# An attention and expert kernel on one core: attention loads released by TensorE's progress, values a step sooner, early weights behind the gathers

## The chip, the cores and the metric

The kernel runs on one core of a Trainium2 chip. The metric is device time in microseconds (us) of one execution; smaller is better. Single launches of one program differ a little, so a time is given as the median of several runs with the lowest and the highest.

## The reference

Eight batches of eight heads, 576 positions, 64 numbers a head. Heads 0 to 3 attend to the last 32 positions (local), heads 4 to 7 to every 32nd position (strided). The rows of the result are tokens, and each goes through one of eight experts.

```python
scores = scale * np.matmul(q, k.transpose(0, 1, 3, 2))
mask_local = (rel >= 0) & (rel < stride)
mask_strided = (rel >= 0) & (pos[None, :] % stride == pos[:, None] % stride)
...
attn = attn / (np.sum(attn, axis=-1, keepdims=True) + 1e-09)
return np.matmul(attn, v).astype(np.float32)
...
logits = x @ w_gate + modality_bias[modality_id]
e_idx = np.argmax(logits, axis=1)
for e in range(E):
    h = np.maximum(x[mask] @ w1[e], 0.0)
    out[mask] = gate_w[mask, None] * (h @ w2[e])
```

## The kernel before

**Two stages.** The attention stage takes about the first 157 us. Behind it the expert stage runs 18 slots of 256 tokens and one half slot; per slot TensorE does the same eight pieces (up, L924, and down, L938), each in three products of high and low parts, and weights come in by indirect DMAs on GpSimd's queue (L811).

**Attention in units and steps.** `units` (L968 to 975) holds 32 units in turn: `Local` (two batches of one local head) and `Strided` (two strided heads of one batch). The loop at L1045 makes one step for each n and works on several units at once. In step n stand the scores of unit n (L380 and L387 for a local, L476 for a strided one), the transposes of the softmaxed scores of unit n-2 (`turn`, L217), the masks of unit n+1 (L368, L469) and the products with the values of unit n-3 (`values`: L420 and L432, or L520). Small pieces of other work are put in between: `pop` runs the joining of finished heads and the routing (`finish_pair`, `route`: tiles xl, xs, lg), and `slow` issues, one each time, scatters of finished token rows to the DRAM table xd (L646), and later the first gathers of tokens and weights (`early`, L989). Between L1041 and L1075 TensorE's order is the order of the code; the other engines' order comes from a scheduler.

**Loads.** They are issued on SyncE's queue (SP), which does one after the other and stands still where one has to wait. A unit's queries and keys are two DMAs of 64 rows (`load_qk`, L324: even partitions at L326, odd ones at L327; tile lqk of a local unit, sqk of a strided one). Each kind has two buffers, so unit n+3 writes the buffer of unit n-1 and waits for its scores. Values are in tile vv for a local unit, also with two buffers, and vs for a strided one. Up to the seventh local unit (`SPREAD`, L31) vv comes in four parts, of which GpSimd copies two on (L360, L361); later ones come from array vl in two. vs is one DMA of 72 rows of 4 KB. In step n stand first the queries and keys of unit n+3, and behind them the values of unit n-1 (L1046 to L1049).

**Waits written by hand.** `paced(ins)` (L219) makes an instruction wait for the TensorE instruction in `recent`, the last one that a helper has noted there: a transpose, a product with values, or a score of a strided unit. Before the change only small work, the scatters and `early` use it. `early` issues weights 0, the two halves of token gather 0, weights 1, the two halves of gather 1, one each time that `slow` comes by.

Of the kernel before, what the change touches and what calls it, by code (L numbers as in the profile page):

```python
# [11 lines left out]
F32 = mybir.dt.float32  # L12
# [8 lines left out]
P = 128  # L21
# [89 lines left out]
def _layout(q, k, v, moe_modality_id, moe_w_gate, moe_modality_bias, moe_w1, moe_w2):  # L111
    q, k, v = (np.asarray(t, np.float32) for t in (q, k, v))

    def local_t(t):
        return t[:, :4].reshape(NBP, 2, 4, S, D).transpose(0, 2, 1, 4, 3).reshape(NBP, 4, 2, D, 18, 32)

    qt, kt = local_t(q), local_t(k)
    vr = v[:, :4].reshape(NBP, 2, 4, 18, 32, D).transpose(0, 2, 1, 3, 4, 5)  # L120
    qkl = np.zeros((NBP, 4, 2, D, 37, 32), np.float32)
    win = np.zeros((NBP, 4, 2, 64, 20, D + 1), np.float32)
    vb = np.zeros((NBP, 4, 2, 32, 9, 2, D + 1), np.float32)
    ve = np.zeros((NBP, 4, 64, 2, D + 1), np.float32)
    vf = np.zeros((NBP, 4, 32, D + 1), np.float32)
    win[..., D] = vb[..., D] = ve[..., D] = vf[..., D] = 1
    vf[..., :D] = vr[:, :, 1, 1]
    for bb in range(2):
        for i in range(18):
            blk = _block(i, bb)  # L130
            qkl[:, :, bb, :, i] = qt[:, :, bb, :, blk]
            qkl[:, :, bb, :, 19 + i] = kt[:, :, bb, :, blk]
            w = win[:, :, i % 2, :, 2 * (i // 2) + bb] if i < 16 else win[:, :, 0, :, 2 * i - 16 + bb]
            w[:, :, 32:, :D] = vr[:, :, bb, blk]
            vb[:, :, i % 2, :, i // 2, bb, :D] = vr[:, :, bb, blk]
            if blk:
                qkl[:, :, bb, :, 18 + i] = kt[:, :, bb, :, blk - 1]
                w[:, :, :32, :D] = vr[:, :, bb, blk - 1]
        for lo in range(2):
            ve[:, :, 32 * lo:32 * lo + 32, bb, :D] = vr[:, :, bb, _block(16 + lo, bb)]  # L140
    qkl = np.stack([qkl[:, :, 1], np.concatenate([qkl[:, :, 0, :, 18:], qkl[:, :, 0, :, :18]], axis=-2)], axis=2)
    qkl = qkl.reshape(NBP, 4, P, 37 * 32)
    vl = win.reshape(NBP, 4, P, 20 * (D + 1))
    vb, ve = vb.reshape(NBP, 4, 2, 32, 18 * (D + 1)), ve.reshape(NBP, 4, 64, 2 * (D + 1))

    def strided_t(t):
        t = t[:, 4:].reshape(B, 2, 2, 18, 32, D).transpose(0, 1, 2, 5, 4, 3)
        return np.ascontiguousarray(t).reshape(B, 2, 2, D, S)

    qs, ks = strided_t(q), strided_t(k)  # L150
    qks = np.stack([np.concatenate([qs[:, :, 1], ks[:, :, 1]], axis=-1), np.concatenate([ks[:, :, 0], qs[:, :, 0]], axis=-1)],
                   axis=2).reshape(B, 2, P, 2 * S)

    vs = v[:, 4:].reshape(B, 2, 2, 18, 4, 2, 4, D).transpose(0, 1, 6, 3, 4, 5, 2, 7)
    vs = np.ascontiguousarray(vs).reshape(B, 2, 72, 1024)

    w1 = np.asarray(moe_w1).reshape(E, 4, P, 8, P).transpose(0, 3, 2, 1, 4).reshape(E, 8, P, 512)
    w2 = np.asarray(moe_w2).reshape(E, 8, P, DM)
    w = np.concatenate([w1, w2], axis=-1).reshape(E, 4, 2, P, 1024).transpose(0, 1, 3, 2, 4).reshape(E * 4 * P, 2048)

    wg = np.zeros((P, 4, 32), np.float32)
    wg[:, :, :E] = np.asarray(moe_w_gate).reshape(4, P, E).transpose(1, 0, 2)
    mod = np.ascontiguousarray(moe_modality_id).astype(np.int64).view(np.int32).reshape(NT, 2)[:, 0]
    mod = mod.reshape(36, P).transpose(1, 0)
    mb = np.broadcast_to(np.asarray(moe_modality_bias).reshape(1, 2 * E), (P, 2 * E))
    cf, cb, tok = _constants()
    nul = np.zeros((1, ROW), np.int32)
    nul[0, DM] = NT
    arrays = {
        "qkl": qkl, "vl": vl, "vb": vb, "ve": ve, "vf": vf, "qks": qks, "vs": vs, "w": w,  # L170
        "wg": wg.reshape(P, 4 * 32), "mod": mod, "mb": mb, "cf": cf, "cb": cb, "tok": tok, "nul": nul.view(np.float32),
    }
    return {n: np.ascontiguousarray(t) for n, t in arrays.items()}
# [20 lines left out]
def attention_moe(ctx: ExitStack, tc: tile.TileContext, a, out):  # L194
    nc = tc.nc
# [125 lines left out]
    for t in ets:  # L321
        nc.vector.memset(t[:], 0.0)

    def load_qk(t, nk, src):  # L324
        w = src.shape[1]
        nc.sync.dma_start(t[0:P:2, nk:nk + w], src[0:64])  # L326
        nc.sync.dma_start(t[1:P:2, 0:w], src[64:128])  # L327

    class Local:

# [1 line left out]
        def __init__(self, bp, h, xt):  # L332
            self.bp, self.h, self.xt, self.n = bp, h, xt, 4 * bp + h

        def load(self):
            n = self.n
            self.qk = lqk[n % 2]
            load_qk(self.qk.rearrange("p x i q -> p (x i q)"), S + 32, a["qkl"][self.bp, self.h])

        def load_values(self):  # L340
            n = self.n
            self.vv = vv = vvs[n % 2]
            w, at = D + 1, (self.bp, self.h)
            for dst, src in (
                (vv[32:64, 0:18, :], a["vb"][*at, 0]),
                (vv[96:128, 0:16, :], a["vb"][*at, 1, :, 0:16 * w]),
                (vv[0:64, 18:20, :], a["ve"][*at]),
                (vv[0:32, 1, :], a["vf"][*at]),
            ) if n < SPREAD else (
                (vv[:, 0:16, :], a["vl"][*at, :, 0:16 * w]),  # L350
                (vv[0:64, 16:20, :], a["vl"][*at, 0:64, 16 * w:]),
            ):
                ins = nc.sync.dma_start(dst, src)
                if n < 2:
                    pin(ins)

        def spread_values(self):
            vv = self.vv
# [12 lines left out]
        def scores(self):  # L371
            n, q, kd = self.n, self.qk[:, 0, 19:37, :], self.qk[:, :, 0:19, :]
            self.ex = ex = lp.tile([P, 9, 64], F32, tag="ex", name=f"ex{n}")
            for half, sp in enumerate(self.sp):
# [9 lines left out]
                if half:  # L384
                    for u in range(4):
                        i = 16 + u // 2
                        nc.tensor.matmul(  # L387
                            sp[32 * u:32 * u + 32, 256:320], q[:, i, :],
                            kd[:, u % 2, i:i + 2, :].rearrange("p i q -> p (i q)"),
                            start=False, stop=True, skip_group_check=True,  # L390
                        )
                mx = lp.tile([P, 5], F32, tag="mx", name=f"mx{n}{half}")[:, :gn]
                nc.vector.tensor_reduce(mx, sp.rearrange("p (g c) -> p g c", g=gn), AX.X, ALU.max)
                e = ex[:, 4 * half:4 * half + gn, :]
# [54 lines left out]
    class Strided:  # L449
# [2 lines left out]
        def __init__(self, b, pr, xc):  # L452
            self.b, self.pr, self.xc, self.n = b, pr, xc, 2 * b + pr

        def load(self):
            n = self.n
            self.qk = sqk[n % 2]
            load_qk(self.qk.rearrange("p i q -> p (i q)"), S, a["qks"][self.b, self.pr])

        def load_values(self):  # L460
            n = self.n
            self.vs = lp.tile([72, 8, 2, D], F32, tag="vs", name=f"vs{n}")
            ins = nc.sync.dma_start(self.vs.rearrange("p g h d -> p (g h d)"), a["vs"][self.b, self.pr])
            if n < 2:
                pin(ins)

        def masks(self):
            self.s = pa(f"ss{self.n}")[:, :288]
# [45 lines left out]
        def values(self):  # L514
            n, eb, vs, b = self.n, self.eb, self.vs, self.b
            for g2 in range(2):
                ot = pa(f"ot{n}{g2}")[:, :288]
                for u in range(4):
                    for h in range(2):
                        recent[:] = [nc.tensor.matmul(  # L520
                            ot[64 * h:64 * h + 64, 72 * u:72 * u + 72],
                            vs[:, 4 * g2 + u, h, :],
                            eb[:, 4 * (2 * h + g2) + u, :, :].rearrange("p t q -> p (t q)"),
                            start=True, stop=True, skip_group_check=True,
                        )]
                base = (b % 2) * S
                dst = self.xc[:, base:base + S].rearrange("p (q r) -> p r q", r=32)[:, 16 * g2:16 * g2 + 16, :]
                nc.scalar.copy(dst, ot.rearrange("p (r q) -> p r q", r=16))
# [459 lines left out]

    def early():  # L989
        for k in range(2):  # L990
            yield
            pin(paced(weights(tables[0][1], 0, k)))
            yield
            n, t, i, xrows = plan[k]
            for xt, ins in token_halves(n, tables[t][0], i, xrows):
                gathered[k] = xt
                pin(paced(ins))
                yield

    def slow():  # L1000
        while calm and next(calm[0], calm) is calm:
# [35 lines left out]

    nu = len(units)
    for i in range(3):
        units[i].load()  # L1040
    man = tc.manual_schedule(engines={mybir.EngineType.PE})  # L1041
    man.__enter__()
    units[0].masks()
    setup = routing_setup()
    for n in range(nu + 3):  # L1045
        if n + 3 < nu:  # L1046
            units[n + 3].load()
        if 1 <= n <= nu:
            units[n - 1].load_values()  # L1049
        if 2 <= n <= nu + 1 and not n % 2:  # L1050
            units[n - 2].spread_values()
        if n < nu:
            units[n].scores()
            if n % 2:
                slow()
            pop(MIDS)
        if 2 <= n <= nu + 1:
            units[n - 2].turn()
        slow()
        if n + 1 < nu:  # L1060
            units[n + 1].masks()
# [83 lines left out]
```

## Time and profile before

| | |
|---|---|
| median of 3 runs | 602.03 us (599.36 to 603.37) |
| the profiled execution, its own time | 597.48 us |
| its span, first to last instruction | 595.4 us |
| mean granted TensorE clock | 0.977 |
| TensorE matmul busy | 564.8 us, 95% |
| VectorE, ScalarE, GpSimd busy | 426.1, 358.7, 244.7 us |
| TensorE busy from 0 to 160 us | 138.2 us |
| TensorE busy from 200 to 560 us | 359.96 of 360 us |

The page gives, for each engine, the share of the span in which it worked (PE is TensorE's matmuls, PEld its weight loads, DVE VectorE, ACT ScalarE, POOL GpSimd, SP SyncE). A chain of waits goes back from the last instruction to whatever released each one; "issue" in it is time in which the engine waited for nothing that the profile shows. A table of windows gives for a stretch of time each engine's busy time and its number of instructions in brackets, then the granted TensorE clock (PEclk, 1.00 is full), the busy share of the 16 DMA engines and the GB/s that they moved. A timeline of a queue (SPq) lists when each DMA was issued, not when its data came.

### The profile page before, as it was taken

To read this page: it belongs to the slowest core of one execution; us is meant where nothing else is said; L and a number is where in the kernel's file an instruction comes from. 1 tells how busy PE (TensorE), PEld (TensorE's weight loads), DVE (VectorE), ACT (ScalarE), POOL (GpSimd) and SP (SyncE) were. 2 spreads that over 40 slices of the span, in tenths; PEclk is the share of its full clock that TensorE was granted. 3 is DMA by queue.
4 is the path that set the end of the run, shared out by engine and by line. 5 is a ranking of instruction groups with operands and counts; after the bars stand their busy time and mean duration, and the time that the engine had idled before them with its cause. 6 is when DMAs were issued, how large, how long until landed. Compare 5 with 4: busy or idle time off the path is not lost.

```text
span 595.4 us, 15277 instructions
## 1 busy us (share of the span) xinstructions
PE 564.8 (95%) x6040; PEld 494.4 (83%) x6040; DVE 426.1 (72%) x1050; ACT 358.7 (60%) x739; POOL 244.7 (41%) x219
## 2 busy tenths in 40 slices
PE   6979888989998999999999999999999999999995
PEld 3767776767887989999899899999998998998984
DVE  6776662957969997767767777777777677677541
ACT  3455664657866566666666666665665666666641
POOL 1413240143757786642543533533534533332220
PEclk9789997989999999999999999999999999999998
DMA  8988895897788855955934823413403438200621
GB/s 275 250 220 217 250 344 189 276 341 258 262 215 210 259 164 164 236 184 129 250 119 125 248 98 74 108 36 73 109 21 87 109 119 252 71 16 22 244 91 38
DMA packets 66669, 100.57 MB, mean 169 GB/s; under 512 B 47775, under 2 KB 49055, under 8 KB 63008
## 3 DMA queue, kind: packets, MB, share of 16 engines
q0 software_dynamic: 19744, 58.57, 29.7%
q1 hardware_dynamic: 46560, 40.56, 27.0%
q8 instruction: 49, 0.80, 0.6%
q10 hardware_dynamic: 288, 0.41, 0.2%
q14 instruction: 28, 0.23, 0.1%
HBM read 121.74 MB, written 19.43 MB: 237 GB/s over the span
## 4 chain that ended last, share of the span: by engine, by line
PE 85%; issue 5%; DVE 4%; DMA 3%; ACT 2%; POOL 1%; SPq 0%; POOLq 0%; ACTq 0%
PE h L924 33%; PE o L938 32%; PE o L420 3%; PE s L380 3%; PE ot L520 3%; PE lg L571 2%; PE xs L217 2%; PE t L217 2%; PE ss L476 1%; PE xl L217 1%; PE ts L217 1%; DMA vv<-in_vb 1%; ACT wh L959 1%; DVE wl L960 1%; DMA lqk<-in_qkl 1%
## 5 line engine op out<-in xcount | busy, mean ns | idle before, releaser
L960 DVE TENSOR_TENSOR wl<-raw,wh 128x512 fp32r<-128x512 f32 x288 | 185.9, 686 | 85.0 <-ACT wh L959 84.9
L959 ACT CAST wh<-raw 128x512 fp32r<-128x512 f32 x288 | 164.0, 618 | 91.4 <-PE o L938 89.6
L924 PE MATMUL h<-xl,wh 128*128 128x256 f32 x576 | 162.1, 282 | 1.4 <-DVE xl L912 1.4
L924 PE MATMUL h<-xh,wh 128*128 128x256 f32 x576 | 163.0, 284 | 0.2 <-ACT xh L911 0.2
L924 PE MATMUL h<-xh,wl 128*128 128x256 f32 x576 | 162.8, 283 | 0.0
L811 POOL DMA_INDIRECT raw<-in_w,wi x72 | 92.7, 1287 | 162.4 <-DVE wl L960 154.1
L924 PEld LDWEIGHTS h<-xl,wh 128*128 128x128 f32 x576 | 108.8, 189 | 8.1 <-DVE xl L912 2.1
L938 PE MATMUL o<-wh,hh 128*128 128x512 f32 x288 | 114.6, 398 | 0.0
L924 PEld LDWEIGHTS h<-xh,wh 128*128 128x128 f32 x576 | 108.4, 189 | 7.1 <-issue 0.6
L938 PE MATMUL o<-wl,hh 128*128 128x512 f32 x288 | 113.6, 395 | 0.0
L938 PE MATMUL o<-wh,hl 128*128 128x512 f32 x288 | 112.2, 395 | 0.0
L924 PEld LDWEIGHTS h<-xh,wl 128*128 128x128 f32 x576 | 108.3, 188 | 0.9
L927 ACT ACTIVATE hh<-h 128x256 fp32r<-128x256 f32 x144 | 55.2, 384 | 55.0 <-PE h L924 52.7
L929 DVE SCALAR_TENSOR_TENSOR hl<-h,hh 128x256 fp32r<-128x256 f32 x144 | 60.3, 419 | 12.5 <-ACT hh L927 12.3
L646 POOL DMA_INDIRECT xd<-xt,posi x36 | 40.4, 1121 | 59.1 <-DVE sms L496 16.5
L938 PEld LDWEIGHTS o<-wh,hl 128*128 128x128 f32 x288 | 53.7, 188 | 11.8
L938 PEld LDWEIGHTS o<-wh,hh 128*128 128x128 f32 x288 | 54.3, 188 | 7.6
L938 PEld LDWEIGHTS o<-wl,hh 128*128 128x128 f32 x288 | 54.3, 189 | 5.8
L946 POOL DMA_INDIRECT out<-y,le x36 | 46.2, 1283 | 24.0 <-ACT y L945 16.1
L792 POOL DMA_INDIRECT fx<-xd,li x36 | 39.2, 1090 | 23.6 <-issue 8.5
L409 ACT COPY et<-t 64x512 f32<-64x512 f32 x32 | 18.5, 579 | 21.1 <-PE t L217 20.7
L420 PEld LDWEIGHTS o<-vv,et 128*64 128x64 f32 x512 | 19.0, 152 | 13.4 <-issue 10.1
(183 smaller groups left out, 687.9 us busy)
## 6 DMA issues: line engine op xcount, KB each, us to landing
lqk<-in_qkl SPq DMA_DIRECT2D x32, 296.0 KB
sqk<-in_qks SPq DMA_DIRECT2D x32, 288.0 KB
vv<-in_vl SPq DMA_DIRECT2D x9, 520.0 KB
vs<-in_vs SPq DMA_DIRECT2D x16, 288.0 KB
raw<-in_w,wi POOLq DMA_INDIRECT x72, 2.5
vv<-in_vb SPq DMA_DIRECT2D x7, 146.2 KB
vv<-in_vb SPq DMA_DIRECT2D x7, 130.0 KB
vv<-in_vl SPq DMA_DIRECT2D x9, 65.0 KB
```

The source lines that it names most:

```text
L217: recent[:] = [nc.tensor.transpose(dst, src, ident)]
L420: recent[:] = [nc.tensor.matmul(os[bb][64 * jj:64 * jj + 64, bb + k, :], et[:, 2 * (k // 2) + bb, 2 * (k % 2) + jj, :, :].rearrange("p g q ...
L646: scattered(bp, paced(nc.gpsimd.indirect_dma_start(xd[0:(bp + 1) * T2, :], IOA(ap=posi[:, i:i + 1], axis=0), xt[:, i, :], None)))
L792: yield xt, fetches(min(xrows // T2, NBP) - 1, nc.gpsimd.indirect_dma_start(xt[:, h, :], None, xd[0:xrows, :], IOA(ap=li[:, s, h:h + 1], a ...
L811: return nc.gpsimd.indirect_dma_start(raws[j].rearrange("p f c -> p (f c)"), None, a["w"], IOA(ap=wi[:, s, j:j + 1], axis=0), bounds_check ...
L924: recent[:] = [nc.tensor.matmul(hp, w[:, a1], x[:, c, :], start=(k == 0), stop=(k == 11))]
L927: nc.scalar.activation(hh[:], hp, AF.Relu)
L929: nc.vector.scalar_tensor_tensor(hl[:], hp, 0.0, hh.bitcast(F32), ALU.max, ALU.subtract)
L938: nc.tensor.matmul(os[h], hx[:, m], w[:, 512:1024], start=(f == 0 and i == 0), stop=(f == 7 and i == 2))
L946: outs.add(nc.gpsimd.indirect_dma_start(out, IOA(ap=le[:, h, 0:1], axis=0), y[:], None, bounds_check=NT - 1, oob_is_err=False))
L959: nc.scalar.copy(wh[:, c], raw[:, c])
L960: nc.vector.tensor_tensor(wl[:, c], raw[:, c], wh[:, c].bitcast(F32), ALU.subtract)
```

## The change

It does five things. The queries and keys are issued one half at a time: for unit n+3 the even partitions behind the scores of unit n, the odd ones behind `turn` of unit n-2, both `paced` (from step 1 on; in step 0 unit 3 is loaded at once). The values of unit n are issued at the head of step n instead of step n+1, ahead of the queries and keys, and `paced` from the third unit of each kind on. The late local values come in two DMAs of 64 rows instead of one of 128. vs is padded from 72 to 80 rows, of which the products read 72. `early` issues both token gathers ahead of both weights. So that `paced` follows the scores of local units too, the last score now sets `recent`.

```diff
-    vs = np.ascontiguousarray(vs).reshape(B, 2, 72, 1024)
+    vs = np.concatenate([vs.reshape(B, 2, 72, 1024), np.zeros((B, 2, 8, 1024), np.float32)], axis=2)
...
-    def load_qk(t, nk, src):
+    def load_qk(t, nk, src, x):
         w = src.shape[1]
-        nc.sync.dma_start(t[0:P:2, nk:nk + w], src[0:64])
-        nc.sync.dma_start(t[1:P:2, 0:w], src[64:128])
+        if x:
+            return nc.sync.dma_start(t[1:P:2, 0:w], src[64:128])
+        return nc.sync.dma_start(t[0:P:2, nk:nk + w], src[0:64])
...
-                (vv[:, 0:16, :], a["vl"][*at, :, 0:16 * w]),
+                (vv[0:64, 0:16, :], a["vl"][*at, 0:64, 0:16 * w]),
+                (vv[64:128, 0:16, :], a["vl"][*at, 64:128, 0:16 * w]),
...
                 if n < 2:
                     pin(ins)
+                else:
+                    paced(ins)
...
-                        nc.tensor.matmul(
+                        recent[:] = [nc.tensor.matmul(
                             sp[32 * u:32 * u + 32, 256:320], q[:, i, :],
...
-            self.vs = lp.tile([72, 8, 2, D], F32, tag="vs", name=f"vs{n}")
+            self.vs = lp.tile([80, 8, 2, D], F32, tag="vs", name=f"vs{n}")
...
     def early():
         for k in range(2):
+            n, t, i, xrows = plan[k]
+            for xt, ins in token_halves(n, tables[t][0], i, xrows):
+                yield
+                gathered[k] = xt
+                pin(paced(ins))
+        for k in range(2):
             yield
             pin(paced(weights(tables[0][1], 0, k)))
-            yield
-            n, t, i, xrows = plan[k]
-            for xt, ins in token_halves(n, tables[t][0], i, xrows):
-                gathered[k] = xt
-                pin(paced(ins))
-                yield
...
     for i in range(3):
-        units[i].load()
+        for x in range(2):
+            units[i].load(x)
...
     for n in range(nu + 3):
-        if n + 3 < nu:
-            units[n + 3].load()
-        if 1 <= n <= nu:
-            units[n - 1].load_values()
+        if not n:
+            for x in range(2):
+                units[3].load(x)
+        if n < nu:
+            units[n].load_values()
         if 2 <= n <= nu + 1 and not n % 2:
             units[n - 2].spread_values()
         if n < nu:
             units[n].scores()
+            if n and n + 3 < nu:
+                paced(units[n + 3].load(0))
             if n % 2:
                 slow()
             pop(MIDS)
         if 2 <= n <= nu + 1:
             units[n - 2].turn()
+        if n and n + 3 < nu:
+            paced(units[n + 3].load(1))
         slow()
```

The first place is SyncE's queue at the start of the program; lqk_84 and lqk_85 are the two buffers of the local units, sqk_86 and sqk_87 those of the strided ones, vv_90 the first buffer of local values. Before:

```order
L326 DMA sqk_87<-in_qks 64x1152
L327 DMA sqk_87<-in_qks 64x1152
L326 DMA lqk_84<-in_qkl 64x1184
L327 DMA lqk_84<-in_qkl 64x1184
L353 DMA vv_90<-in_vb 32x1170
L353 DMA vv_90<-in_vb 32x1040
```

And of the change:

```order
L328 DMA sqk_87<-in_qks 64x1152
L327 DMA sqk_87<-in_qks 64x1152
L355 DMA vv_90<-in_vb 32x1170
L355 DMA vv_90<-in_vb 32x1040
L355 DMA vv_90<-in_ve 64x130
L355 DMA vv_90<-in_vf 32x65
L467 DMA vs_192<-in_vs 80x1024
L328 DMA lqk_84<-in_qkl 64x1184
```

The first values moved ahead of the second load of lqk_84, which has to wait for unit 0's scores; the first vs moved there too.

The second place is the same queue in a later step, with what each row waits for (PE is a TensorE instruction, DMAHW with a number an earlier DMA on one of eight semaphores). Before:

```order
L353 DMA vv_91<-in_vl 128x1040 [waits DMAHW4_49,PE_49]
L353 DMA vv_91<-in_vl 64x260 [waits DMAHW5_49,PE_49]
L326 DMA lqk_85<-in_qkl 64x1184 [waits DMAHW6_49,PE_49]
L327 DMA lqk_85<-in_qkl 64x1184 [waits DMAHW7_49]
L463 DMA vs_1841<-in_vs 72x1024 [waits DMAHW0_49,PE_49]
L326 DMA sqk_87<-in_qks 64x1152 [waits DMAHW1_49,PE_49]
L327 DMA sqk_87<-in_qks 64x1152 [waits DMAHW2_49]
```

And of the change:

```order
L355 DMA vv_91<-in_vl 64x1040 [waits DMAHW4_49,PE_49]
L355 DMA vv_91<-in_vl 64x1040 [waits DMAHW5_49]
L355 DMA vv_91<-in_vl 64x260 [waits DMAHW6_49,PE_49]
L328 DMA sqk_86<-in_qks 64x1152 [waits DMAHW7_49,PE_49]
L327 DMA sqk_86<-in_qks 64x1152 [waits DMAHW0_49,PE_49]
L467 DMA vs_1706<-in_vs 80x1024 [waits DMAHW1_49,PE_49]
L328 DMA lqk_85<-in_qkl 64x1184 [waits DMAHW2_49,PE_49]
L327 DMA lqk_85<-in_qkl 64x1184 [waits DMAHW3_49,PE_49]
```

Every second half now has a TensorE instruction of its own to wait for, and values of a later unit stand beside the same queries and keys. There are nine more DMAs, the second parts of the late local values.

The third place is GpSimd's queue at the end of the attention stage; raw is a tile of weights, fx_0 and fx_1 are the first two gathers of tokens. Before:

```order
L811 DMA raw_2704<-in_w,wi_2225 128x2048 [waits DVE_49,PE_49]
L792 DMA fx_0_2787<-xd,li_2217 128x528 [waits DVE_49,PE_49]
L792 DMA fx_0_2787<-xd,li_2217 128x528 [waits PE_49]
L811 DMA raw_2904<-in_w,wi_2225 128x2048 [waits PE_49]
L792 DMA fx_1_2975<-xd,li_2217 128x528 [waits PE_49] x2
```

And of the change:

```order
L798 DMA fx_0_2619<-xd,li_2223 128x528 [waits DVE_49,PE_49]
L798 DMA fx_0_2619<-xd,li_2223 128x528 [waits PE_49]
L798 DMA fx_1_2796<-xd,li_2223 128x528 [waits PE_49] x2
L817 DMA raw_2914<-in_w,wi_2231 128x2048 [waits PE_49]
L817 DMA raw_2985<-in_w,wi_2231 128x2048 [waits PE_49]
```

The first weights moved behind four gathers, the second behind two. TensorE's rows are the same, in the same order, up to the first expert slots, where the scheduler has put some pieces of neighbouring slots the other way round.

More of the change, by code (lines that the diff above doesn't have):

```diff
@@ L333, in __init__, with load @@
             self.bp, self.h, self.xt, self.n = bp, h, xt, 4 * bp + h
-        def load(self):
+        def load(self, x):
             n = self.n
             self.qk = lqk[n % 2]
-            load_qk(self.qk.rearrange("p x i q -> p (x i q)"), S + 32, a["qkl"][self.bp, self.h])
+            return load_qk(self.qk.rearrange("p x i q -> p (x i q)"), S + 32, a["qkl"][self.bp, self.h], x)
         def load_values(self):
@@ L390, in scores @@
                             start=False, stop=True, skip_group_check=True,
-                        )
+                        )]
                 mx = lp.tile([P, 5], F32, tag="mx", name=f"mx{n}{half}")[:, :gn]
@@ L453, in __init__, with load @@
             self.b, self.pr, self.xc, self.n = b, pr, xc, 2 * b + pr
-        def load(self):
+        def load(self, x):
             n = self.n
             self.qk = sqk[n % 2]
-            load_qk(self.qk.rearrange("p i q -> p (i q)"), S, a["qks"][self.b, self.pr])
+            return load_qk(self.qk.rearrange("p i q -> p (i q)"), S, a["qks"][self.b, self.pr], x)
         def load_values(self):
             n = self.n
-            self.vs = lp.tile([72, 8, 2, D], F32, tag="vs", name=f"vs{n}")
+            self.vs = lp.tile([80, 8, 2, D], F32, tag="vs", name=f"vs{n}")
             ins = nc.sync.dma_start(self.vs.rearrange("p g h d -> p (g h d)"), a["vs"][self.b, self.pr])
@@ L465, in load_values @@
                 pin(ins)
+            else:
+                paced(ins)
         def masks(self):
@@ L521, in values @@
                             ot[64 * h:64 * h + 64, 72 * u:72 * u + 72],
-                            vs[:, 4 * g2 + u, h, :],
+                            vs[0:72, 4 * g2 + u, h, :],
                             eb[:, 4 * (2 * h + g2) + u, :, :].rearrange("p t q -> p (t q)"),
```

## The prediction

> **What bounds the kernel now.** I read the page first, then a table of windows by stage, then the chain of waits over the attention stage, and for its odd pieces the windows between them. The stages first (us; then busy time of PE, PEld, DVE, ACT, POOL with the number of instructions; granted clock, DMA share, GB/s):
>
> ```profile
> 0.00:160.00 160.00, 138.20 (x3302) 111.11 (x3303) 109.41 (x406) 91.86 (x211) 50.08 (x64) 0.93 0.85 262
> 200.00:560.00 360.00, 359.96 (x2289) 325.51 (x2288) 271.68 (x514) 227.37 (x445) 162.52 (x130) 1.00 0.46 128
> ```
>
> From 200 us on TensorE never rests and has its full clock: nothing there can be won by moving loads. The attention stage is different. TensorE rests 160 - 138.2 = 21.8 us in it, and its clock is 0.93. So the question is where those 21.8 us lie. The chain of waits (start, length, what) has the answer:
>
> ```profile
> 9.41 6.33 DMA vv<-in_vb
> 15.90 1.04 POOL vv L360
> 17.00 1.00 POOL vv L361
> 18.04 2.00 PE o L420 x30
> ...
> 31.47 1.37 issue
> ...
> 43.08 1.64 issue
> ...
> 49.39 1.15 issue
> ...
> 70.53 1.67 issue
> ...
> 86.47 0.61 PE o L420 x15
> 87.08 3.98 issue
> 91.06 1.24 PE o L420 x17
> ```
>
> ```profile
> 114.27 0.83 issue
> ...
> 119.36 1.71 issue
> ...
> 132.84 0.65 issue
> ```
>
> One wait is for data: the first values, issued at 9.41, let TensorE go on at 18.04. All the others are called "issue", 13.00 us in sum, and they break off in the middle of a group: at 87.08 fifteen of 32 equal products are done, the other seventeen follow 3.98 us later, though all read the same tiles. No tile was missing. What was missing shows when one counts instructions (PE and PEld) between such breaks:
>
> ```profile
> 43.08:49.39 6.31, 4.67 (x125) 4.01 (x126) 4.51 (x13) 2.95 (x8) 2.04 (x2) 1.00 0.92 243
> 70.53:87.08 16.55, 14.88 (x378) 12.52 (x377) 11.16 (x36) 10.56 (x26) 7.36 (x8) 0.90 0.93 308
> 87.08:119.36 32.28, 26.93 (x630) 21.00 (x631) 19.37 (x92) 16.52 (x40) 4.66 (x6) 0.89 0.76 245
> ```
>
> 125 + 126 = 251; 755 is 3 times 252; 1261 is 5 times 252. Breaks come only at whole multiples of about 251 instructions. On the page stands a queue with as many packets as that makes:
>
> ```profile
> PE 564.8 (95%) x6040; PEld 494.4 (83%) x6040; DVE 426.1 (72%) x1050; ACT 358.7 (60%) x739; POOL 244.7 (41%) x219
> q8 instruction: 49, 0.80, 0.6%
> ```
>
> 12,080 instructions through 49 packets are 247 each. So TensorE's program itself comes by DMA, a block of some 250 instructions at a time, and a break is a block that came late. In the expert stage a block lasts about 20 us (4,577 instructions in 360 us), in attention 6,605 instructions are 26 blocks in 160 us, 6.1 us each: only there can it be late. And there the DMA engines are full; the break of 3.98 us falls into the fullest stretch:
>
> ```profile
> 77.00:92.00 15.00, 11.02 (x319) 9.47 (x315) 7.79 (x23) 8.80 (x21) 5.76 (x6) 0.95 0.97 348
> 20.00:140.00 120.00, 106.19 (x2583) 86.41 (x2582) 77.05 (x279) 69.70 (x164) 33.92 (x37) 0.92 0.84 255
> ```
>
> Each long rest has a second price, a halved clock soon after (the 0.50 in the last columns):
>
> ```profile
> 15.50:22.20 6.70, 5.46 (x84) 4.26 (x82) 4.55 (x12) 1.19 (x3) 2.83 (x3) 0.50 0.95 265
> 32.60:35.80 3.20, 2.95 (x38) 2.24 (x38) 2.21 (x5) 2.87 (x8) 0.29 (x1) 0.50 0.69 191
> 73.50:76.80 3.30, 3.30 (x48) 2.65 (x38) 2.86 (x10) 1.31 (x3) 2.10 (x2) 0.50 0.93 254
> 90.60:97.30 6.70, 6.24 (x66) 3.79 (x70) 1.15 (x6) 0.76 (x2) 1.25 (x2) 0.50 0.70 246
> 121.30:124.60 3.30, 3.30 (x68) 2.80 (x64) 1.74 (x13) 0.00 (x0) 0.95 (x1) 0.50 1.02 344
> ```
>
> Half of the busy time in each is lost: 2.7, 1.5, 1.65, 3.1 and 1.65 us. They follow the start and the breaks of 1.37, 1.67, 3.98 and 1.71 us; those of 1.64, 1.15, 0.83 and 0.65 have none behind them.
>
> **The change part by part.** *The start.* SyncE's queue shows why the first values are late (issue times):
>
> ```profile
> 5.89 0.56 SPq L327 DMA_DIRECT2D sqk<-in_qks  x1
> 8.25 0.47 SPq L326 DMA_DIRECT2D lqk<-in_qkl  x1
> ```
>
> The queue stands from 6.45 to 8.25, because lqk's second load waits for unit 0's scores, and the values are behind it. Now they stand ahead of it and can go out at about 7.0, 2.4 us sooner; with the same 6.33 us under way, and GpSimd's two copies of 2.1 us, the values are ready near 15.5. TensorE's own work ahead of them ends then at 16.3:
>
> ```profile
> 15.63 0.69 PE L368 MATMUL s<-cb_sb 128*128 128x256 bf16 x2
> ```
>
> So the products begin at 16.3 instead of 18.04: -1.7 us. With 2 us less rest the second half of that slow-clock period should go, 1.35 us. I take -3; bounds 0 (another engine holds TensorE until 18) and -5 (the whole period of 2.7 us goes and the block that follows comes in time).
>
> *The blocks.* Before, a buffer that comes free lets both halves out at once:
>
> ```profile
> 81.48 0.47 SPq L326 DMA_DIRECT2D lqk<-in_qkl  x1
> 82.01 0.63 SPq L327 DMA_DIRECT2D lqk<-in_qkl  x1
> ```
>
> A pair is 2 x 64 x 4,736 B = 0.606 MB, at the 348 GB/s of that stretch 1.74 us of DMA time; values add up to 0.6 MB, as much again. Afterwards a half, 0.87 us, is let out behind the scores, the other half some TensorE work later, the values at the head of the step. A block that is asked for behind such a burst then waits 0.87 us (the other half) to 2.6 us (half and values) less. I take 1 us, near the low end, since the scatters on GpSimd's queue, which are let out as before, stay in the way. Each break is shortened by 1 us or to nothing: 1.37, 1.64, 1.15, 1.67, 3.98 and 1.71 by 1, 0.83 and 0.65 altogether, 7.5 us in sum. Bounds: 0, if the depth of the queue does not matter, and 13.0, all breaks.
>
> *The clock.* The breaks of 1.37, 1.67 and 1.71 us become 0.4 to 0.7, the size of those that cost no clock: 1.5 + 1.65 + 1.65 = -4.8 us. The one of 3.98 stays near 3 and keeps its 3.1. Bounds 0 and -7.9.
>
> *Given back.* The same bytes go in less time. From 20 to 140 us the DMA engines are busy for 0.84 x 120 = 101 us; with 12 us less that is 0.93 of the stretch, and where it is 0.97 already there is little to win. I put +2 on it, an estimate between 0 (a spread load queues less) and +10 (TensorE gains only until the engines are full, which gives most of it back).
>
> *Loads one step later.* Queries and keys of unit n+3 were let out by the scores of unit n-1, and are now by work of step n. A step is 4.8 us, by these two pieces, twelve pairs of steps apart:
>
> ```profile
> 23.26 1.15 PE ot L520 x32
> ...
> 138.18 1.15 PE ot L520 x32
> ```
>
> The second half still has two and a half steps, 12 us, against the 6.33 us that the values took under a full queue. I cost it at 0; that cover is what the slower rival takes away. Behind a waiting half on SyncE's queue stand only the next values, which have three steps and more.
>
> *Small parts, at 0 together.* Nine more DMAs on SyncE's queue are nine issues of about 0.6 us while it waits for TensorE anyway. vs grows by 32 KB, 0.1 us of DMA time, sixteen times. [...]
>
> *The early weights.* They go out in the place of the second gather:
>
> ```profile
> 147.36 0.94 POOL L792 DMA_INDIRECT fx<-xd,li  x1 [0.92 <-PE rk L638]
> 149.17 0.94 POOL L792 DMA_INDIRECT fx<-xd,li  x1 [0.86 <-PE ts L217]
> ```
>
> ```profile
> 157.17 4.27 ACT wh L959 x8
> ```
>
> A tile of weights is 1.05 MB, 4 us at the stage's 262 GB/s: the first lands near 152, the second near 156, and ScalarE's casts begin at 157.17 and come to the second tile 2.1 us later. I take 0; if the scatters behind take turns with them, up to +3.
>
> **Sum:** -3 - 7.5 - 4.8 + 2 = -13.3 us against the profiled execution's 597.48, so 584.2. That execution lies 4.55 us under the median of the runs, 602.03, so I forecast 588.7, rounded to 589.
>
> **The rivals.** *The depth of the queue does not matter.* If a block's packet has to pass only what is in the engines, it waits as before as long as any load runs; then only the start is won, 602 - 3 = 599. For it: a break of 1.64 us at 43.08 stands where 243 GB/s, no peak, are moved. Against it: the longest break is in the fullest stretch, and none is in the expert stage. [...]
>
> *The DMA engines become the bound.* The breaks go, but the loads can't follow, and half of the gain returns as waits for lqk or sqk: -13.3 becomes -6, 596. For it: 0.97 in the fullest stretch. Against it: 0.84 over the whole.
>
> *Slower: the engines run dry between releases.* A load is let out only when TensorE gets there. From 20 to 140 us they are idle 0.16 x 120 = 19.2 us; there are 25 steps with three releases, 75. If each leaves a gap of over 19.2 / 75 = 0.26 us, loads fall behind TensorE and it waits for lqk and sqk. At 0.4 us, less than one issue of 0.47, that is 30 - 19.2 = +10.8, less 3 at the start: 610. For it: 0.89 or more of DMA share in several windows. Against it: loads that are late pile up, and a queue that has piled up leaves no gaps.
>
> **How the numbers follow.** The forecast gets 0.60 (its own range 579 to 597, from all breaks and most of the clock to a third of both), the full engines 0.12, depth without effect 0.18, gaps 0.10. A measurement of this kernel can tell about 1%, 6 us, from no change. Faster by over 1%, under 596: the forecast nearly whole, 0.59, and half of the full engines, 0.06: 0.65. Within 1%: 0.01 + 0.06 + 0.18 = 0.25. Slower: 0.10. The range 579 to 603 leaves out the gaps, 0.10, and about 0.08 at its ends.
>
> **What would show it.** Right: the first products with values begin at 16 to 17 us; the "issue" pieces of the attention stage fall from 13.0 to 4 to 7 us, still at multiples of some 251 instructions; the clock from 0 to 160 us rises to 0.95 or more; the expert stage begins some 12 us sooner and runs at the same pace. Wrong: breaks of the same size (depth does not matter), or PE waits whose releaser is a DMA of lqk, sqk, vv or vs after 20 us (gaps or full engines), or a rest at the first slot that ends with raw (the early weights).

## The result, and the profile after

The change made the kernel a little slower: 604.36 us in the median (600.23 to 608.96, 16 runs) against 600.67 (597.18 to 605.89, 16 runs) of the kernel before on the same chip, a ratio of 1.0065 with a 95% interval of 1.0038 to 1.0092. The forecast was 589, faster. The profiled execution after took 600.23 us (span 597.9, mean clock 0.983); the one before 597.48 (595.4, 0.977).

First the windows of the kernel after, with the same columns as before:

```profile
0.00:160.00 160.00, 136.63 (x3293) 109.61 (x3293) 107.12 (x402) 91.08 (x209) 50.48 (x64) 0.95 0.91 267
20.00:140.00 120.00, 106.29 (x2659) 87.05 (x2653) 77.48 (x285) 71.92 (x169) 32.91 (x38) 0.95 0.90 264
200.00:560.00 360.00, 360.00 (x2290) 325.91 (x2289) 272.76 (x528) 228.07 (x447) 159.71 (x130) 1.00 0.46 128
```

TensorE rests 160 - 136.63 = 23.4 us in the attention stage, where it had rested 21.8. The column to look at is the last but one: from 20 to 140 us the DMA engines are busy 0.90 of the time instead of 0.84, a rise of 7%, for 264 GB/s instead of 255, a rise of 3.5%. They work longer for each byte. From 200 us on the expert stage is as it was.

The breaks are still there. Two views of the kernel after: rows of the chain of waits (start, length, what), and then what TensorE waited for from 20 to 140 us (us in total, times, the longest), where "issue" is again the break between blocks of its program:

```profile
31.39 2.04 issue
...
42.27 0.84 issue
...
47.77 1.75 issue
...
69.50 2.22 issue
...
115.51 2.18 issue
```

```profile
PE o L424 <- issue: 5.7, 3, 2.2
PE ss L482 <- issue: 4.8, 4, 2.0
PE s L384 <- issue: 2.0, 3, 0.8
PE s L391 <- issue: 0.9, 1, 0.9
```

These rows add up to 13.4 us. The "issue" rows of the same view of the kernel before add up to 13.4 us too:

```profile
PE o L420 <- issue: 7.4, 3, 4.0
PE ss L476 <- issue: 2.9, 3, 1.4
PE s L380 <- issue: 1.6, 1, 1.6
PE s L387 <- issue: 0.8, 1, 0.8
PE lg L571 <- issue: 0.7, 1, 0.7
```

After the change no row names a DMA of lqk, sqk, vv or vs, so the loads are not late. The breaks still stand at whole numbers of blocks, here one block and three:

```profile
42.27:47.77 5.50, 4.66 (x126) 3.98 (x125) 4.03 (x13) 2.96 (x8) 2.11 (x3) 1.00 0.97 278
69.50:88.73 19.23, 15.69 (x378) 12.91 (x377) 11.60 (x37) 10.95 (x27) 7.88 (x8) 0.91 1.01 313
```

126 + 125 = 251 and 378 + 377 = 755, which is three times 252. The traces say it more directly than the counts: from 20 to 140 us each of the breaks of over 0.6 us, eight before and nine after, ends 1.27 to 1.61 us after a packet of the instruction queue q8 has landed. The packet behind the break of 3.98 us before, which ends at 91.06, began only at 88.58 and landed at 89.53.

Half clock stands at the start and behind two of the long rests, those at 69.50 and 115.51; behind those of 2.04 us at 31.39 and 1.75 us at 47.77 there is none:

```profile
14.90:21.70 6.80, 5.92 (x87) 4.73 (x88) 5.52 (x15) 1.33 (x3) 2.71 (x4) 0.50 1.04 269
72.90:76.30 3.40, 3.40 (x50) 2.75 (x40) 3.07 (x10) 1.21 (x3) 2.03 (x2) 0.50 0.98 245
117.30:124.10 6.80, 6.41 (x93) 5.34 (x95) 3.56 (x19) 1.32 (x3) 1.92 (x2) 0.50 1.02 311
```

Three periods stand where five stood, with 15.7 us of busy time instead of 21.3. Half of the difference, 2.8 us, is what the clock gave in this one execution.

### The profile page after: what moved, and what is told of

It reads as the page before. It is cut to its first block, busy times and chain, and to the rows that moved or that the text cites. A ratio compares the mean times of both kernels' runs of the same rounds, so it can differ in the third digit from the quotient of the medians.

```text
span 597.9 us, 15313 instructions
## 1 busy us (share of the span) xinstructions
PE 565.7 (95%) x6040; PEld 494.5 (83%) x6040; DVE 426.0 (71%) x1050; ACT 359.2 (60%) x739; POOL 240.9 (40%) x219
## 4 chain that ended last, share of the span: by engine, by line
PE 86%; issue 6%; DVE 5%; DMA 2%; ACT 0%; POOL 0%; SPq 0%; POOLq 0%; DVEq 0%
PE h L930 34%; PE o L944 32%; PE o L424 3%; PE ot L526 3%; PE s L384 3%; PE ss L482 2%; PE t L217 2%; PE xl L217 1%; DVE wl L966 1%; PE ts L217 1%; PE xs L217 1%; PE lg L577 1%; DMA lqk<-in_qkl 1%; DMA xd<-xt,posi 1%; PE o L436 1%
## 5 line engine op out<-in xcount | busy, mean ns | idle before, releaser
L817 POOL DMA_INDIRECT raw<-in_w,wi x72 | 89.3, 1241 | 162.0 <-DVE wl L966 152.5
L652 POOL DMA_INDIRECT xd<-xt,posi x36 | 37.3, 1037 | 60.7 <-PE s L384 13.9
L952 POOL DMA_INDIRECT out<-y,le x36 | 49.3, 1368 | 28.6 <-ACT y L951 21.3
```

The lines of the kernel that those rows point to most:

```text
L652: scattered(bp, paced(nc.gpsimd.indirect_dma_start(xd[0:(bp + 1) * T2, :], IOA(ap=posi[:, i:i + 1], axis=0), xt[:, i, :], None)))
L817: return nc.gpsimd.indirect_dma_start(raws[j].rearrange("p f c -> p (f c)"), None, a["w"], IOA(ap=wi[:, s, j:j + 1], axis=0), bounds_check ...
L952: outs.add(nc.gpsimd.indirect_dma_start(out, IOA(ap=le[:, h, 0:1], axis=0), y[:], None, bounds_check=NT - 1, oob_is_err=False))
```

## The experiments

Fourteen kernels ran. Their ratios are to the kernel before, measured in turns on the same chip, with 95% intervals. The last column is the sum of TensorE's "issue" rows from 20 to 140 us, read as above from the one profiled execution of each.

| kernel | what it is | ratio | breaks, us |
|---|---|---|---|
| changed | all five parts | 1.0065 (1.0038 to 1.0092) | 13.4 |
| e1 | changed, early order as before | 1.0127 (1.0078 to 1.0175) | 15.0 |
| e2 | before + early order | 0.9986 (0.9938 to 1.0033) | 7.9 |
| e3 | before, most queries and keys not loaded | 0.9759 (0.9690 to 0.9828) | 3.5 |
| e4, e8, e13 | before, at most 2, 4, 6 loads out | 1.1264, 1.0625, 1.0269 | 0, 0, 5.3 |
| e5 | before + values sooner | 0.9980 (0.9937 to 1.0023) | 12.5 |
| e6 | before + paced halves of queries and keys | 0.9985 (0.9939 to 1.0031) | 9.7 |
| e7 | before + layout (padding and split) | 1.0123 (1.0087 to 1.0158) | 12.9 |
| e9 | before + padding | 1.0018 (0.9981 to 1.0054) | 12.2 |
| e10 | before + split into halves | 1.0119 (1.0062 to 1.0175) | 14.9 |
| e11 | changed, layout as before | 0.9989 (0.9951 to 1.0028) | 12.0 |
| e12 | before + split into even and odd partitions | 1.0014 (0.9978 to 1.0049) | 11.5 |
| e14 | changed, split into even and odd partitions | 0.9980 (0.9942 to 1.0017) | 10.8 |

A caution on the last column: e2 differs from the kernel before in nothing that moves an attention load, and shows 7.9 us where that one shows 13.4. The executions of e5 (604.42 us) and e12 (606.96 us) are among the longest of their runs. A single execution says no more than that. The intervals of the ratios carry the verdicts.

**Is it the early weights?** My first suspicion was the entry of the expert stage. In the profiled pair the changed kernel is ahead at the local scores of one unit (the recorded text below calls them strided), and behind at the first group of 33 products of the expert stage, which the prediction had some 12 us sooner. Before, then after:

```profile
113.17 1.01 PE s L380 x32
...
190.20 4.18 PE h L924 x33
```

```profile
108.61 1.01 PE s L384 x32
...
193.45 4.18 PE h L930 x33
```

e1 takes the new order out of the changed kernel, and e2 puts it alone into the kernel before:

```diff
     def early():
         for k in range(2):
+            yield
+            pin(paced(weights(tables[0][1], 0, k)))
+            yield
             n, t, i, xrows = plan[k]
             for xt, ins in token_halves(n, tables[t][0], i, xrows):
-                yield
                 gathered[k] = xt
                 pin(paced(ins))
-        for k in range(2):
-            yield
-            pin(paced(weights(tables[0][1], 0, k)))
+                yield
```

> The changed kernel, with the early weights and gathers back in their old order (weights 0, gather 0, weights 1, gather 1). Theory A, my own now: the attention breaks are as long as before because letting loads out in halves does not lower what is queued at the DMA engines; the early order costs nothing, so this stays within 2 us of the changed kernel. Rival C: the changed kernel gains some 3 to 4 us in the attention loads, as its strided scores at 108.6 us against 113.2 show, and loses them and 4 more at the entry of the expert stage, because the first weights go out behind four gathers; then this kernel is 4 to 8 us faster than the changed one, and 1 to 4 us faster than the one before. Where to look: the first product of the expert stage that is repeated 33 times, at 190.20 us before and 193.45 after the change.

> The kernel before, with only the new order of the early weights and gathers. Theory A: no difference, within 2 us of the kernel before. Rival C: 3 to 8 us slower, with the whole loss between 140 and 190 us, at the entry of the expert stage, and the same breaks in the attention stage as before.

Measured: 1.0127 and 0.9986. Without the new order the changed kernel is no faster, and the new order alone costs nothing that can be told. Rival C fell. Theory A had e1 within 2 us of the changed kernel; by the ratios it lies 0.6%, 3.7 us, above it, with intervals that overlap, so if anything the new order helps. What turned the lead at 108 us into a lag at 193 stays open: e11 and e14, which lose nothing in the ratios, show the same (109.62 to 193.32, 107.36 to 192.42).

**Do the breaks come from the traffic?** e3 leaves out the loads of queries and keys of every unit but the first two of each kind, so it computes the later units from old contents:

```diff
-    def load_qk(t, nk, src):
+    def load_qk(t, nk, src, n):
         w = src.shape[1]
+        if n > 1:
+            return
...
```

> The kernel before, with the loads of queries and keys left out for all units but the first two of each kind (the later units use the old contents again); some 17 of the 42 MB of the first 160 us are gone. If the breaks between TensorE's program blocks come from the traffic in front of the block's packets, the breaks from 20 to 140 us fall from 13 us to under 4, the mean time from the asking for a block to its packet from 4 us to 1 to 2, the half-clock periods behind them go, and the time falls by 10 to 17 us. If the breaks belong to the fetching itself and not to the traffic, the breaks stay at 10 to 15 us and the time falls by less than 4.

Measured: 0.9759, about 14 us faster. The windows and the waits of TensorE from 20 to 140 us in e3:

```profile
20.00:140.00 120.00, 112.00 (x2967) 91.98 (x2960) 88.00 (x347) 80.11 (x189) 38.57 (x41) 0.99 0.53 166
```

```profile
PE o L422 <- issue: 1.7, 3, 0.7
PE s L389 <- issue: 1.4, 1, 1.4
...
PE ot L522 <- issue: 0.4, 1, 0.4
```

With a DMA share of 0.53 the breaks are 3.5 us and the clock is 0.99. That the breaks come from the traffic, and that the half clock goes when they go, is shown. The rest of what e3 won in the attention stage it gave back at the next limit, the first weights of the expert stage (chain of waits):

```profile
148.18 11.32 DMA raw<-in_w,wi
```

**Does the depth matter, and can it be had lower?** e4, e8 and e13 hold the loads back until the second, fourth or sixth load before has landed:

```diff
+DEPTH = 2
...
+    flying = []
+
+    def behind(ins):
+        if len(flying) >= DEPTH:
+            tc.add_manual_dep(ins.ins, flying[-DEPTH].ins.name, ...)
+        flying.append(ins)
+        return ins
...
-        nc.sync.dma_start(t[0:P:2, nk:nk + w], src[0:64])
+        behind(nc.sync.dma_start(t[0:P:2, nk:nk + w], src[0:64]))
...
```

> The kernel before, where each load of attention waits until the second load before it on SyncE's queue has landed, so that two are under way at most and the queued depth is bounded. Theory A (depth is what a block waits behind, and the halves did not lower it): the time from the asking for a block to its packet falls from 4 us to 2 or less, the breaks from 13 us to under 6; the time falls by 4 to 10 us unless loads come late, which would show as waits of TensorE for DMAs of lqk, sqk, vv or vs. [...]

> The kernel before, where each load of attention waits until the fourth load before it has landed (the kernel with two was 12.6 percent slower, its DMA share 0.52 from 20 to 140 us, and TensorE waited for lqk, sqk, vv and vs). At most some 1.2 MB are out. If a bound on the depth can be had without running dry, the breaks fall under 8 us and the time is within 1 percent of before or faster. If the loads need the depth to keep 255 GB/s, TensorE still waits for them and the time is 2 to 6 percent longer, with a DMA share of 0.65 to 0.8.

> The kernel before, where each load of attention waits for the landing of the sixth load before it. With four the breaks fell to 1 us, but TensorE waited for the loads and the time was 6 percent longer; with two 13 percent. If there is a depth that shortens the breaks and still feeds TensorE, this one is within 1 percent of before or faster, with breaks of 3 to 8 us from 20 to 140 us and few waits for lqk, sqk, vv and vs. If the breaks can only be had at the price of late loads, because at 255 GB/s some 0.7 MB must be out anyway, the breaks go back toward 8 to 13 us as the waits for loads go, and the time is 1 to 4 percent longer.

Measured: 1.1264 (1.1181 to 1.1347), 1.0625 (1.0544 to 1.0707) and 1.0269 (1.0199 to 1.0339). The windows from 20 to 140 us of the kernels with two, four and six:

```profile
20.00:140.00 120.00, 84.19 (x1649) 68.92 (x1649) 50.11 (x159) 44.82 (x101) 24.75 (x27) 0.73 0.52 151
```

```profile
20.00:140.00 120.00, 92.36 (x2201) 75.16 (x2200) 64.97 (x234) 57.77 (x135) 26.43 (x29) 0.88 0.62 191
```

```profile
20.00:140.00 120.00, 101.93 (x2479) 83.03 (x2482) 72.61 (x273) 66.02 (x154) 32.26 (x35) 0.91 0.75 231
```

The loads move 151, 191 and 231 GB/s, against 255 before. With four, TensorE's waits in that stretch hold no "issue" row (the chain of waits has one break of 1.07 us) and name the loads and their copies in its place:

```profile
PE o L431 <- POOL vv L371: 7.8, 4, 3.4
PE o L431 <- DMA vv<-in_vf: 6.8, 4, 2.9
PE o L431 <- DMA vv<-in_vl: 3.9, 2, 3.4
...
PE s L391 <- DMA lqk<-in_qkl: 1.2, 1, 1.2
```

With two and four the breaks are gone, with six they are 5.3 us, and each bound made the loads late and cost more than the 13 us that were to be had. None of the three depths gives both short breaks and loads in time. They lower the rate with the depth, so by themselves they don't part depth from rate.

The trace can be asked further. For each block I took the amount that was out when it was asked for: bytes of all loads, scatters and gathers issued until then, less the bytes whose packets had begun; and how long it then took until the block's own packet began. When a block is asked for is not recorded. I set it some 300 TensorE instructions before the block's own first one, which is an assumption, and the waits below rest on it. For it: in the expert stage of the kernels before and after, where the DMA share is 0.46, a block's packet begins 250 to 297 instructions ahead, so it was asked for no later than that. Over 286 blocks after 20 us, in twelve executions at full depth:

```
out when asked (MB)   under 0.25   0.25-0.5   0.5-0.75   0.75-1   1-1.5   over 1.5
blocks                    51          57         71        48       48       11
mean wait (us)           2.37        3.15       3.77      4.36     5.66     7.31

without paced halves (6 executions, 143 blocks): 0.66 MB out, wait 4.10 us
with paced halves    (5 executions, 118 blocks): 0.70 MB out, wait 4.05 us
without most queries and keys (e3, 25 blocks):   0.41 MB out, wait 2.62 us
```

The wait grows by 3.0 us per MB (correlation 0.69). With the asking set at 360 instructions ahead the slope is 2.5, so its size is an estimate. What is out does go with how long a block waits; a correlation shows no more. But the paced halves leave as much out as before: the amount varies by 0.4 MB from block to block, so 0.66 and 0.70 can't be told apart. The mean breaks of the same executions are 12.1 us without and 12.2 us with paced halves.

**The parts, one at a time.** e5 has only the values sooner, none of them paced, e6 only the paced halves, e7 only the layout; each takes its hunks of the change into the kernel before.

```diff
-        if n + 3 < nu:
+        if not n:
+            units[3].load()
+        if n < nu:
+            units[n].load_values()
+        if n and n + 3 < nu:
             units[n + 3].load()
-        if 1 <= n <= nu:
-            units[n - 1].load_values()
```

> The kernel before, with only the values of each unit issued a step sooner, ahead of queries and keys as in the changed kernel, but nothing paced and no padding. Theory A (what a block of program waits behind is the amount of loads out at that moment): loads that are out sooner queue deeper; the start gains 0.75 us, as in the changed kernel, where the first products with values begin at 17.3 us against 18.0, and the breaks grow by 2 to 5 us, so the time is 0 to 5 us longer than before. My forecast's term for the start: 3 us faster than before. Rival D (the loss of the changed kernel comes from the pacing alone): within 2 us of before or faster.

```diff
         if n < nu:
             units[n].scores()
+            if n and n + 3 < nu:
+                paced(units[n + 3].load(0))
...
             units[n - 2].turn()
+        if n and n + 3 < nu:
+            paced(units[n + 3].load(1))
```

> The kernel before, with only the queries and keys issued a half at a time behind TensorE's progress; values, padding and early order as before. My forecast's term for the blocks: breaks 7.5 us shorter and the clock's half periods fewer, 8 to 12 us faster than before. Theory A: the mean amount out when a block is asked for stays at 0.5 MB, the breaks at 11 to 16 us in the attention stage, the time within 3 us of before. Rival D: the pacing itself costs, 3 to 6 us slower than before.

```diff
-                (vv[:, 0:16, :], a["vl"][*at, :, 0:16 * w]),
+                (vv[0:64, 0:16, :], a["vl"][*at, 0:64, 0:16 * w]),
+                (vv[64:128, 0:16, :], a["vl"][*at, 64:128, 0:16 * w]),
...
-            self.vs = lp.tile([72, 8, 2, D], F32, tag="vs", name=f"vs{n}")
+            self.vs = lp.tile([80, 8, 2, D], F32, tag="vs", name=f"vs{n}")
```

> The kernel before, with only the layout of the values: strided values padded to 80 rows, late local values in two DMAs of 64 rows. Theory A and my forecast: within 2 us of before (nine more issues, 0.5 MB more of 42). Rival E (the layout makes the loss: the DMA share of 20 to 140 us went from 0.84 to 0.90 while the GB/s rose only from 255 to 264): 3 to 6 us slower, with a DMA share of 0.88 or more in that stretch at about 255 GB/s.

Measured: 0.9980, 0.9985 and 1.0123. Neither the values nor the pacing do anything that can be told from nothing. The trace of e6 also has what the slower rival spoke of, late loads:

```profile
PE s L381 <- DMA lqk<-in_qkl: 4.2, 2, 2.9
...
PE ss L477 <- DMA sqk<-in_qks: 1.2, 1, 1.2
```

That is 5.4 us of waits for queries and keys, beside 9.7 us of breaks. The kernel before, e11, e14 and the changed kernel have no such row, but e2, whose attention loads are those of before, has one of 2.0 us, so this too is one execution's word. The layout, which the forecast and Theory A had at zero, costs 1.2%, more than the whole change. Rival E stands.

**Padding or split, and why.** e9 has only the padding, e10 only the split, e12 the split with other partitions:

```diff
-                (vv[:, 0:16, :], a["vl"][*at, :, 0:16 * w]),
+                (vv[0:128:2, 0:16, :], a["vl"][*at, 0:128:2, 0:16 * w]),
+                (vv[1:128:2, 0:16, :], a["vl"][*at, 1:128:2, 0:16 * w]),
```

e11 is the changed kernel with the layout as before, e14 the changed kernel with the split of e12.

> The kernel before, with only the strided values padded from 72 to 80 rows. The layout as a whole cost 1.2 percent, 7 us. [...] Theory Q (the padding is the cause of the loss): 5 to 8 us slower. My forecast: no difference.

> The kernel before, with only the late local values in two DMAs of 64 rows, partitions 0 to 63 and 64 to 127. Theory P: their packets of 4,160 bytes take a median of 230 ns or more instead of 161, since each of the two DMAs reaches half of the partitions, and the time is 4 to 7 us longer. Theory Q (padding): within 2 us of before.

> The kernel before, with the late local values in two DMAs of 64 rows as in the split kernel, but even partitions in the one and odd ones in the other, as queries and keys are loaded. Same number of DMAs, same bytes. Theory P: the packets of 4,160 bytes are back at 160 to 185 ns and the time is within 2 us of before. Rival R (a second DMA, its issue and its rows make the loss, whichever partitions it writes): as long as the split by halves, 4 to 7 us slower.

> The changed kernel without its layout: strided values of 72 rows, late local values in one DMA of 128 rows; values sooner, paced halves and the new early order stay. If the parts add up, -0.2, -0.15 and -0.14 percent of the three measured alone make 0.5 percent, 3 us faster than before, and 4 to 8 us faster than the changed kernel. My forecast of 13 us for these parts would be 2 percent. If the parts hinder each other, within 1 us of before or slower.

> The changed kernel with one line pair altered: its two late parts of the local values hold even and odd partitions instead of the lower and the upper half. If the halves were all that it lost, the time is within 2 us of the kernel before (the other parts together measured 0.9989) and 4 to 8 us shorter than the changed kernel; the packets of 4,160 bytes are back at a median of 160 to 185 ns. If something in the changed kernel besides the halves costs, it stays 3 us or more above the kernel before.

Measured: padding 1.0018, split into halves 1.0119, split into even and odd 1.0014, changed without the layout 0.9989, changed with even and odd 0.9980. It is the halves. What they do stands in one line of the DMA view from 60 to 160 us, where the late local values run: the packets of the plain loads, their MB, and their time as a share of 16 engines. Before, then split into halves (e10), then split into even and odd (e12):

```profile
q1 hardware_dynamic: 5384, 17.76, 55.8%
```

```profile
q1 hardware_dynamic: 5575, 17.93, 62.4%
```

```profile
q1 hardware_dynamic: 5560, 17.91, 56.9%
```

Nearly the same bytes, in two kernels that issue the same number of DMAs, take 62.4 us of all the engines by halves, and 56.9 by even and odd partitions. The changed kernel and e14 differ in the same way:

```profile
q1 hardware_dynamic: 5816, 18.72, 65.0%
```

```profile
q1 hardware_dynamic: 5692, 18.25, 60.0%
```

That is 3.47 us per MB and 3.29. Packet by packet: the rows of 4,160 bytes, most of which are late local values, take a median of 161 ns before and in e2, e9, e11, e12 and e14, and of 234 to 256 ns in e7, e10 and the changed kernel (the means, which long packets raise in both, are 211 ns before and 263 in e10). At 161 ns a row moves at 25.8 GB/s, at 256 at 16.3. The windows rows of the split into halves and of the split into even and odd show the price, 0.89 of DMA share against 0.83 for the same 255 GB/s:

```profile
20.00:140.00 120.00, 104.37 (x2522) 84.69 (x2515) 74.06 (x274) 67.94 (x158) 32.53 (x35) 0.92 0.89 255
```

```profile
20.00:140.00 120.00, 106.85 (x2568) 86.62 (x2560) 75.68 (x279) 70.38 (x164) 32.63 (x36) 0.92 0.83 255
```

e12 alters two things at once, the partitions that a DMA writes and the rows of the DRAM array that it reads, every other one too. The queries and keys part them: each of their DMAs reads 64 neighbouring rows and writes every other partition, and in the kernel before its packets of 4,736 bytes take a median of 182 ns, 26.0 GB/s. So neighbouring rows are no hindrance; it is the partitions.

The packets of 4,096 bytes take a median of 159 ns with padding (e9), 175 before. The padding brings nothing and costs nothing that can be told (1.0018).

How the longer DMA time becomes 7 us of TensorE I can't split further. e10's single execution has 14.9 us of breaks against 13.4 and a clock of 0.91 against 0.93 from 0 to 160 us, both in the right direction and both within the scatter of single executions.

## Why the prediction was wrong

**The view of the bound was right.** TensorE's program comes in blocks of some 251 instructions, a break ends some 1.4 us after the block's packet has landed (1.27 to 1.61 before and after), and blocks are late while the loads run: e3 took 17 MB of the traffic away, and most of the breaks (13.4 us became 3.5), the half clock behind them (the mean clock from 20 to 140 us went from 0.92 to 0.99) and 14 us went.

**The blocks, the step that failed.** "A block that is asked for behind such a burst then waits 0.87 us (the other half) to 2.6 us (half and values) less": this gave -7.5 us and, behind it, -4.8 of the clock. Its first half holds as far as the estimate above goes, by which a block waits 3.0 us longer for each MB that is out. Its second half, that pacing leaves less in front of a block, does not: 0.66 MB are out without paced halves, 0.70 with them, and the mean breaks are 12.1 and 12.2 us. Why the amount stays is my reading and not tested: pacing spreads the moments of release, but the loads still have to move at some 260 GB/s through engines that are busy 0.84 of the time. I read a shallower queue off the order of the issues, when the trace of before already had the amount out, which could have told that a pair released at once was only one of its parts. Alone, the pacing measures 0.9985; with the sooner values and the early order 0.9989 and, with the padding and the even and odd split too, 0.9980. That is about 1 us, not told from nothing, for everything that was to bring 13. For these parts, without the halves, the rival "the depth of the queue does not matter" came out near in time (599 from 602), but for another reason than its own: by the estimate above waits do rise with what is out, 3.0 us per MB, and what is out did not change (0.66 and 0.70 MB). It was near by luck.

**The clock, -4.8.** The term had breaks of 1.37, 1.67 and 1.71 us shrink to 0.4 to 0.7 and lose their half clock. The breaks did not shrink, so its ground is gone. The length of a break does not decide alone either: that of 1.64 us had no half clock behind it before, and those of 2.04 and 1.75 us have none after. The 2.8 us that the clock gave in the profiled execution is no sign for the term, since this execution is no faster.

**The start.** The values went out at 6.49 us (forecast 7.0) and were ready at 15.31 (15.5). That part was right. The group of 32 products, of which before two ran at 16.99 and thirty from 18.04, began at 17.29 and not at 16.3. Rows of TensorE at the start of the kernel after, with the idle time before each in brackets, and of GpSimd's copies:

```profile
14.23 0.29 PE L482 MATMUL ss<-sqk 128*18 128x36 f32 x10 [1.17 <-issue]
15.78 1.04 PE L217 MATMUL ts<-cf_sb,ens 128*72 128x128 f32 x4 [1.26 <-DVE ens L504]
16.61 0.68 PE L372 MATMUL s<-cb_sb 128*128 128x256 bf16 x2
17.22 1.03 PE L424 MATMUL o<-vv,et 128*64 128x65 f32 x14
```

```profile
14.32 0.99 POOL L365 COPY vv<-vv 32x975 f32<-32x975 f32 x1
```

TensorE's own work in front was later than before: a break of 1.17 us in the middle of the strided scores (0.74 before), then the softmax behind them. The second half of the slow-clock period stayed (14.9 to 21.7). So 0.75 us was won where -3 was put, and 0.9980 over the whole can't be told from nothing.

**Small parts, "at 0 together".** This term was mis-sized. The split into halves costs 1.2%, about 7 us. I had costed nine issues on SyncE's queue and not the packets. The same DMA count with even and odd partitions measures 1.0014, so neither the issues nor the second DMA cost anything that can be told; which partitions a DMA reaches does. A packet of 4,160 bytes takes a median of 161 ns from one DMA over all 128 partitions and from two of 64 rows over every other partition, and of 234 to 256 ns from two over the lower and the upper half. Why the halves are slower was not shown; the runs show only which partitions.

**The early weights, 0:** right, 0.9986. **Loads one step later, 0, and engines run dry:** no DMA is among TensorE's waits after the change from 20 to 140 us, so putting them low was right for the whole; the 5.4 us in e6 would say, if they came again, that the cover was thinner than the two and a half steps reckoned.

**Given back, +2:** nothing was won that could be given back, so no run shows this term.

**The balance.** Forecast -13.3 us; measured +0.65%, 3.9 us. Of the 17 us between them some 7 are the halves and some 12 what the other parts did not bring; the sum is over by 2, which is within the intervals: inside the changed kernel the halves cost 5 us (1.0065 against 0.9980), on the kernel before 7.

## What to carry to other kernels

Before you spread transfers in time, read from the trace how much is out on average and what rate the consumer needs: here, with the engines busy 0.84 of the time, moving the releases moved nothing that can be told (0.66 and 0.70 MB out), fewer bytes did (e3, 0.9759), and slower packets cost (e10, 1.0119). When a DMA is cut in two, try even and odd partitions (161 ns a packet here) and not the lower and upper half (234 to 256 ns), and look at the packets' time per MB, not only at the number of issues. And measure the parts that were costed at nothing as well as the main one: here the main one did nothing that can be told, and one of those decided the sign.

## What the runs showed that I had not expected

The fetch of TensorE's program is a real cost at full traffic: 8 to 15 us of breaks in 120 us, from waits of, by my estimate, 2.0 us plus 3.0 us per MB out. Two DMAs of 64 rows each take a median of 234 to 256 ns a packet of 4,160 bytes on the lower and upper half of the partitions, and 161 on even and odd ones. And a bound on the loads in flight costs a lot here: 13%, 6% and 3% for two, four and six; six loads, of 0.25 MB in the mean, gave 231 GB/s where the kernel before moved 255.
